# A state-space layer and a feed-forward block on one core: the second half of a matrix is loaded later, and one group of products trades places with another

## The chip, the cores and the metric

The kernel runs on one core of a Trainium2 chip. The metric is the device time of one execution in microseconds (us), the median of several runs. All times along the program are counted from the first instruction of one profiled execution.

## The reference

Sequence length 2048, width 512, 128 states, hidden width 1792, everything in float32. Cut to what matters:

```python
mod = (_silu(c) @ w_mod).reshape(c.shape[0], 6, 1, -1)   # sa, ca, ga, sb, cb, gb
h = _layernorm(x) * (1 + ca) + sa
x = x + ga * _A_ref(h, ...)        # K from A, B, C; y = irfft(rfft(u) * rfft(K)) + u * Dskip
h = _layernorm(x) * (1 + cb) + sb
x = x + gb * _B_ref(h, ...)
...
def _B_ref(x, w1, b1, w2, b2):
    h = x @ w1 + b1
    r = jnp.where(h > 0, h, 0)
    return (r * r) @ w2 + b2
```

So there is first a long convolution along the sequence, by Fourier transforms, and then a feed-forward block with a squared ReLU.

## The kernel before

The kernel has two halves. In the first (to about 283 us) the convolution's filter and the input are brought into the frequency domain and multiplied. In the second, which the change touches, the result is brought back into rows of the sequence and goes through the feed-forward block.

**The inverse.** `inverse(n)` for n of 0 to 7 computes two of the 16 tiles of rows (a tile has 128 rows of 512). TensorE multiplies with matrices in the tile `i2c`: `inverse(n)` reads its blocks 8n to 8n+7, so n of 0 to 3 read the first half of `i2c` (blocks 0 to 31) and n of 4 to 7 the second (32 to 63). The results of `inverse(1)` go to the four PSUM banks `tb` (shown as ps and kg), those of all the others to the four banks `accs` (tg). VectorE adds the input rows (n below 4, line 1106) or VectorE and ScalarE copy the banks (line 1108) into `x2`. `statistics` (lines 1113 to 1118) and `normalised` (ScalarE, line 1124) make the layer norm of a tile, four transposes (line 1129) bring it into banks, and `modulated` (lines 1134 and 1136) scales these into the operands of the feed-forward block.

**The load.** `i2_load(j0, j1, after)` loads blocks j0 to j1 of `i2c` in transfers of eight blocks, 256 KB each. It first lets ScalarE copy one element of `after` into the target (line 991), so that the transfers, which come after this write, cannot begin before `after` is there.

**The first product.** For each pair of 512-row groups (k = 0 and k = 2, with k+1), and for each j of 0 to 6, `first_half` and `second_half` make the products with two column blocks of w1 by seven products in place of eight ("11", "21", "t2", "t3", "t1", "t4", "22"). Each is a call of `three`, six matmuls of float32r parts (lines 1173, 1175 and 1177). `second_half` gets three banks a, c and e; for j of 2 on a is tb[0], c is tb[2], e is tb[3]:

```python
first_half(k, j, tb[0], tb[1], cs_[0])
second_half(k, j, tb[0], tb[2], tb[3], [2 * j - 1, 2 * j])
```

`first_half` writes "11" into tb[0] and copies it to c0 on ScalarE (line 1184). "t2" is then added to what stands in tb[0]. Between the products of t1 and t4 stand two calls of `ffn2`, the products with w2 (lines 1215 to 1217), 12 matmuls each.

**The order.** The order of instructions on each engine is not that of the code. `keep_order` sorts all instructions with a model of their costs and ties them in that order; `hurry(mark, ns)` adds a number of nanoseconds from the table `HURRY` to the urgency of all instructions since `mark`. A changed number, or a changed place in the code, can therefore move other instructions too. TensorE's products that go through `turn` keep the order of the code.

Of the kernel before, what the change touches and what calls it, by code (L numbers as in the profile page):

```python
# [27 lines left out]
def j_of(s, g):  # L28
    return 8 * (s // 2) + 4 * (g // 2) + 2 * (s % 2) + g % 2
# [18 lines left out]
    "GH6H.f..f.fggg.gg.7g.hghhhg"  # L48
).split(".")
HURRY = (  # L50
# [308 lines left out]
def tile_adaln_ssm_ffn(  # L359
# [71 lines left out]
    def in_parts(name, parts):  # L431
        for dst, src in parts:
            whole[nc.sync.dma_start(dst, src).ins.name] = name
# [183 lines left out]
    def hurry(start, ns):  # L617
        urgent.update((i.name, ns) for i in list(nc.cur_bb.bb.instructions)[start:])
# [370 lines left out]
    def i2_load(j0, j1, after):  # L989

        nc.scalar.copy(i2c[:, j0, 0, 0:1], after)
        in_parts(f"inverse {j0}", [(i2c[:, j : j + 8], i2v[:, j : j + 8]) for j in range(j0, j1, 8)])
# [91 lines left out]
    x2 = zj[0].rearrange("p c (s q) d -> p s q c d", q=4)  # L1084
# [3 lines left out]
    def turn(pe):  # L1088
        in_turn.update(x.ins.name for x in pe)

    def inverse(n):
        banks = [t[:, 0:256].rearrange("p (i c d) -> p i c d", i=2, c=NC) for t in (tb if n == 1 else accs)]
        for i in range(2):
            for r in range(2):
                for q in range(4):
                    qs = slice(32 * q, 32 * q + 32)
                    for g in range(4):
                        j = j_of(2 * n + i, g)
                        m = nc.tensor.matmul(  # L1099
                            banks[q][32 * g : 32 * g + 32, i], i2c[qs, j, r], zj[r][qs, :, j],  # L1100
                            start=(r == 0), stop=(r == 1))
                        whole[m.ins.name] = f"inverse {n} {i}"
        for q in range(4):
            y = x2[:, 2 * n : 2 * n + 2, q]
            if n < 4:
                nc.vector.tensor_add(y, cd4[n // 2][:, 2 * (n % 2) : 2 * (n % 2) + 2, q], banks[q])
            else:
                (nc.vector.tensor_copy if q % 2 else nc.scalar.copy)(y, banks[q])

    def statistics(s, n=2):  # L1110
        rs = slice(s, s + n)
        for k in range(s, s + n):
            nc.vector.bn_stats(sts[k % 4], x2[:, k])
            nc.vector.bn_aggr(mv[:, k, :], sts[k % 4])
        nc.scalar.activation(rstd2[:, rs], mv[:, rs, 1], AF.Sqrt, bias=epsb)
        nc.vector.reciprocal(rstd2[:, rs], rstd2[:, rs])
        if on_act(s):
            nc.vector.scalar_tensor_tensor(mv[:, rs, 1], mv[:, rs, 0], -1.0, rstd2[:, rs], op0=ALU.mult, op1=ALU.mult)
# [3 lines left out]
    def normalised(s, xn, tps):  # L1122
        if on_act(s):
            nc.scalar.activation(d4(xn), x2[:, s], AF.Identity, scale=rstd2[:, s : s + 1], bias=mv[:, s, 1:2])
        else:
            nc.vector.tensor_scalar(
                d4(xn), x2[:, s], mv[:, s, 0:1], rstd2[:, s : s + 1], op0=ALU.subtract, op1=ALU.mult)
        m = s % 4
        return [nc.tensor.transpose(tp[:, 128 * m : 128 * m + 128], xn[:, 128 * q : 128 * q + 128], ident) for q, tp in tps]

    def modulated(k, q, tp):
        h = h32[k % 2][:, q]
        if q % 2:
            nc.vector.tensor_scalar(h, tp, cbc[:, q : q + 1], sbc[:, q : q + 1], op0=ALU.mult, op1=ALU.add)
        else:
            nc.scalar.activation(h, tp, AF.Identity, bias=sbc[:, q : q + 1], scale=cbc[:, q : q + 1])
        if k % 2 == 0 or q > 1:
            o = ops[("11", "21", "", "22")[k % 2 * 2 + q // 2]]
            split(o[:, 0, q % 2], o[:, 1, q % 2], h)
# [19 lines left out]
    def squares(k, t, c, src=None):  # L1159
        nc.scalar.activation(c, c if src is None else src, AF.Relu, bias=b1c[:, t : t + 1])  # L1160
        if k % 2:
            nc.scalar.activation(rst[:, t], c, AF.Square)
        else:
            h, l = r2_slot(k, t)
            nc.scalar.activation(h, c, AF.Square)
            nc.scalar.activation(c, c, AF.Square)
            nc.vector.tensor_sub(l, c, h.bitcast(F32))  # L1167

    def three(ps, dst, wi, op, start, stop, on=False):
        o = ops[op]  # L1170
        pe = []
        for kt in range(2):
            pe.append(nc.tensor.matmul(  # L1173
                ps, dst[:, 0, wi, kt], o[:, 0, kt], start=start and kt == 0, stop=False, skip_group_check=on))
            pe.append(nc.tensor.matmul(ps, dst[:, 1, wi, kt], o[:, 0, kt], start=False, stop=False, skip_group_check=on))  # L1175
        for kt in range(2):
            pe.append(nc.tensor.matmul(  # L1177
                ps, dst[:, 0, wi, kt], o[:, 1, kt], start=False, stop=stop and kt == 1, skip_group_check=on))
        turn(pe)
# [9 lines left out]
    def second_half(k, j, a, c, e, between):  # L1189
        dst = sets[j % 2]  # L1190
        c1, c2, c3 = quarters(more[:, 0:2048])[1:]
        t = 2 * j
        three(a, dst, 4, "t2", False, True, True)
        nc.scalar.copy(c1, a)
        three(c, dst, 5, "t3", True, True)
        nc.vector.tensor_add(c3, c1, c)
        three(e, dst, 3, "t1", True, True)
        nc.vector.tensor_add(c3, c3, e)  # L1198
        squares(k + 1, t + 1, c3)
        for n in between:  # L1200
            ffn2(k, n, accs)
        three(c, dst, 2, "t4", False, True, True)
        nc.vector.tensor_add(c2, c1, c)
        squares(k, t + 1, c2)
        three(e, dst, 6, "22", False, True, True)
        nc.vector.tensor_add(c1, c1, e)
        squares(k + 1, t, c1)
# [11 lines left out]
    def ffn2(k, t, to):  # L1219
        n = uses.index((k, t))  # L1220
        w2_ready(n + 2)
        product2(k, t, n, to)
# [23 lines left out]

    mark = len(nc.cur_bb.bb.instructions)
    inverse(0)
    i2_load(32, 64, x2[:, 0, 0, 0, 0:1])
    inverse(1)  # L1250
    for s in range(4):
        if s % 2 == 0:
# [6 lines left out]
    for n in range(2, 8):  # L1259
        if n == 5:  # L1260
            mark = len(nc.cur_bb.bb.instructions)
            for s in range(4, 8):
                if s % 2 == 0:
                    statistics(s)
                normalised(s, xts[s], list(enumerate(accs)))
            for q in range(4):
                modulated(1, q, accs[q])
            hurry(mark, HURRY[49])
            mark = len(nc.cur_bb.bb.instructions)
        inverse(n)  # L1270
        if n in (3, 7):
            hurry(mark, HURRY[6 if n == 3 else 48])
            mark = len(nc.cur_bb.bb.instructions)
# [4 lines left out]
    for k in (0, 2):  # L1278
# [15 lines left out]
        w1_load(2)  # L1294
        w1_load(3)
        second_half(k, 0, tb[0], tb[1], tb[3], [0, 2])
        for _ in w1_set(2, nc.gpsimd):
            pass
        second_half(k, 1, tb[2], tb[1], tb[3], [1])
        for j in range(2, 7):  # L1300
            if j < 6:
                for _ in w1_set(j + 1):
                    pass
            if j < 5:
                w1_load(j + 2)
            if k == 0 and j in (3, 5):
                ss = range(8, 12) if j == 3 else range(12, 16)
                mark = len(nc.cur_bb.bb.instructions)
                for s in ss:
                    nc.sync.dma_start(xos[s % 4], xt[s])  # L1310
                    nc.vector.tensor_add(x2[:, s], x2[:, s], d4(xos[s % 4]))
                    if s % 2:
                        statistics(s - 1)
                hurry(mark, HURRY[55])
            gate_rows(range(4 * k + 2 * j - 4, 4 * k + min(2 * j - 2, 8)))
            first_half(k, j, tb[0], tb[1], cs_[0])
            second_half(k, j, tb[0], tb[2], tb[3], [2 * j - 1, 2 * j])
# [31 lines left out]
        n = uses.index((k + 1, NF - 2))  # L1349
# [59 lines left out]
```

## Time and profile before

| | us |
|---|---|
| runs: median, lowest, highest | 617.12, 617.1, 618.1 |
| the profiled execution | 617.67 |
| its span, first to last instruction | 615.9 |
| TensorE busy in the span | 562.1 |
| VectorE busy | 494.9 |
| ScalarE busy | 418.6 |
| GpSimd busy | 246.7 |

The profile has one line for each engine: PE is TensorE's matmuls, PEld its weight loads, DVE VectorE, ACT ScalarE, POOL GpSimd, SP SyncE, which issues the transfers. A row of the timeline gives start, duration, engine, line, operation, what it writes and reads, the count, and in brackets the idle time before it and what ended that. "issue" stands where an engine waited for nothing that the profile shows. In a row of windows each engine has its busy time and the count of its instructions, then come TensorE's granted clock (1.00 is full speed), the share of the DMA engines that was busy, and GB/s.

### The profile page before, as it was taken

Reading aid. Unit: us, or ns where it says so; the run is one execution under the profiler, and the core shown is the slowest. Engines: PE = TensorE matmul, PEld = TensorE weight load, DVE = VectorE, ACT = ScalarE, POOL = GpSimd, SP = SyncE. Lnnn points to the kernel's source line nnn. Section 1 sums busy time; section 2 is a strip of 40 time slices with the busy share of each in tenths; the row PEclk is TensorE's granted clock in tenths of the full one; section 3 lists DMA queues with packets and bytes.
Section 4 is the critical chain, followed back from the end, with each engine's and each line's share of the span. In section 5 each row is a group of like instructions: output and inputs, shape, how many; then the busy total and the mean of one; then the engine's idle time right before and its main releaser. Section 6 shows DMA issues by size and latency. Waiting matters only on the chain.

```text
span 615.9 us, 21264 instructions
## 1 busy us (share of the span) xinstructions
PE 562.1 (91%) x9238; PEld 484.3 (79%) x9238; DVE 494.9 (80%) x870; ACT 418.6 (68%) x747; POOL 246.7 (40%) x202
## 2 busy tenths in 40 slices
PE   1347998999999999997799999999999999999996
PEld 1235988899899999996677778888888878888885
DVE  6899978999998999945798998547999976654744
ACT  5688869979967678553576866666766766666540
POOL 5549998999998799280004100000000400000000
PEclk9999999999999999998799999999999999999999
DMA  8916041240404401576008131113521532111431
GB/s 307 403 30 202 9 73 31 44 73 4 71 4 72 71 6 27 125 167 224 3 11 278 40 120 35 34 36 99 192 85 55 167 104 69 35 38 40 144 104 69
DMA packets 33133, 57.02 MB, mean 93 GB/s; under 512 B 5520, under 2 KB 14608, under 8 KB 31888
## 3 DMA queue, kind: packets, MB, share of 16 engines
q1 hardware_dynamic: 32752, 55.53, 31.6%
q8 instruction: 72, 1.18, 0.8%
q14 instruction: 21, 0.17, 0.1%
q10 hardware_dynamic: 288, 0.13, 0.1%
HBM read 43.07 MB, written 4.19 MB: 77 GB/s over the span
## 4 chain that ended last, share of the span: by engine, by line
PE 67%; DVE 14%; ACT 9%; issue 4%; DMA 3%; POOL 2%; SPq 1%; DVEq 0%; ACTq 0%; POOLq 0%
PE ps L749 8%; PE ps L903 8%; PE ps L759 7%; PE kg L884 4%; PE ps L1173 4%; PE ps L1175 4%; PE ps L1177 4%; PE tg L1215 3%; PE tg L1217 3%; PE tg L1216 3%; PE tg L1099 2%; PE ps L1217 2%; PE ps L1216 2%; PE ps L1215 2%; DMA work<-w 2%
## 5 line engine op out<-in xcount | busy, mean ns | idle before, releaser
L1036 POOL TENSOR_TENSOR work<-work 128x256 f32<-128x256 f32 x4 | 3.3, 837 | 196.7 <-DVE t2t L1167 134.3
L1010 DVE TENSOR_TENSOR w2t<-rw,w2t 128x512 fp32r<-128x512 f32 x53 | 37.9, 717 | 38.8 <-ACT w2t L1009 38.5
L759 PE MATMUL ps<-xy,t_sb 128*64 128x64 f32 x2048 | 65.9, 223 | 1.0 <-DVE xy L894 1.0
L759 PEld LDWEIGHTS ps<-xy,t_sb 128*64 128x64 f32 x2048 | 63.4, 138 | 2.4 <-DVE xy L894 1.2
L1009 ACT CAST w2t<-rw 128x512 fp32r<-128x512 f32 x53 | 32.8, 619 | 44.6 <-PE kg L1217 21.7
L903 PE MATMUL ps<-e_sb,xy 128*64 128x128 f32 x1024 | 61.0, 274 | 1.9 <-DVE xy L894 1.2
L903 PEld LDWEIGHTS ps<-e_sb,xy 128*64 128x64 f32 x1024 | 56.3, 139 | 3.1 <-DVE xy L894 1.4
L1160 ACT ACTIVATE more<-more,b1c 128x512 f32<-128x512 f32 x54 | 38.9, 720 | 26.4 <-DVE more L1198 15.9
L1215 PE MATMUL tg<-w2t,t2t 128*128 128x512 f32 x112 | 43.9, 392 | 0.5 <-DVE t2t L1167 0.5
L1216 PE MATMUL tg<-w2t,t2t 128*128 128x512 f32 x112 | 43.6, 389 | 0.0
L1217 PE MATMUL tg<-w2t,t2t 128*128 128x512 f32 x112 | 43.6, 389 | 0.0
L894 DVE TENSOR_TENSOR xy<-ps,xy 128x512 f32<-128x512 f32 x64 | 39.9, 681 | 0.5 <-PE ps L759 0.4
L1009 ACT CAST wset<-work 128x512 fp32r<-128x512 f32 (+2 forms) x36 | 24.6, 690 | 22.1 <-DMA work<-w 13.1
L1173 PE MATMUL ps<-opt,wset 128*128 128x512 f32 x84 | 34.1, 405 | 2.4 <-ACT more L1184 2.4
L840 POOL TENSOR_TENSOR llph<-lo,big 128x1024 int32<-128x1024 int32 x16 | 34.3, 2144 | 3.7 <-ACT tg L852 3.6
L840 POOL TENSOR_TENSOR rtlph<-lo,big 128x1024 int32<-128x1024 int32 x16 | 34.4, 2151 | 3.4 <-ACT tg L852 2.8
L749 PE MATMUL ps<-d_sb,ksb 128*64 128x128 f32 x512 | 33.8, 276 | 2.0 <-ACT tg L850 1.4
L1215 PE MATMUL ps<-w2t,t2t 128*128 128x512 f32 x84 | 33.4, 398 | 0.0
L1217 PE MATMUL ps<-w2t,t2t 128*128 128x512 f32 x84 | 32.8, 391 | 0.0
L1175 PE MATMUL ps<-opt,wset 128*128 128x512 f32 x84 | 32.8, 391 | 0.0
L1216 PE MATMUL ps<-w2t,t2t 128*128 128x512 f32 x84 | 32.7, 390 | 0.0
L749 PE MATMUL ps<-d_sb,big 128*64 128x128 f32 x512 | 32.1, 274 | 0.1
(287 smaller groups left out, 1640.1 us busy)
## 6 DMA issues: line engine op xcount, KB each, us to landing
rw<-w SPq DMA_DIRECT2D x53, 256.0 KB, 2.7
xy<-xy SPq DMA_DIRECT2D x64, 128.0 KB, 4.1
xy<-xt SPq DMA_DIRECT2D x24, 256.0 KB, 5.4
work<-w SPq DMA_DIRECT2D x12, 512.0 KB, 4.3
out_dram<-more SPq DMA_DIRECT2D x14, 256.0 KB, 2.2
xy<-w_mod SPq DMA_DIRECT2D x3, 1024.0 KB, 9.9
xy<-w_mod SPq DMA_DIRECT2D x12, 256.0 KB, 3.5
t_sb<-c_t SPq DMA_DIRECT2D x1, 2048.0 KB, 15.3
```

Source lines behind the costliest of these rows:

```text
L749: nc.tensor.matmul(ps[64 * r : 64 * r + 64, 128 * i : 128 * i + 128], src[:, i], d1_sb[:, r], start=True, stop=True)
L759: nc.tensor.matmul(ps[64 * r : 64 * r + 64, 64 * i : 64 * i + 64].rearrange("p (h q t) -> p q h t", h=2, t=2), t2_sb[:, 8 * g + i, r], src ...
L840: nc.gpsimd.tensor_tensor(ph.rearrange("p d r (a b) -> p (d r) a b", a=4), bc(low_phase[:, us].rearrange("p d r b -> p (d r) b"), 2, 4), b ...
L894: nc.vector.tensor_mul(product_piece(y, g), ps, piece(x, g))
L903: nc.tensor.matmul(ps[64 * m : 64 * m + 64, 128 * i : 128 * i + 128], pairs(y)[:, g, i // 2, 64 * m : 64 * m + 64, i % 2], e1_sb[:, h], st ...
L1009: nc.scalar.copy(hi_, raw_)
L1160: nc.scalar.activation(c, c if src is None else src, AF.Relu, bias=b1c[:, t : t + 1])
L1173: pe.append(nc.tensor.matmul(ps, dst[:, 0, wi, kt], o[:, 0, kt], start=start and kt == 0, stop=False, skip_group_check=on))
L1175: pe.append(nc.tensor.matmul(ps, dst[:, 1, wi, kt], o[:, 0, kt], start=False, stop=False, skip_group_check=on))
L1215: nc.tensor.matmul(to[m], l[:, xs], hi_, start=(t == 0), stop=False),
L1216: nc.tensor.matmul(to[m], h[:, xs], lo_, start=False, stop=False),
L1217: nc.tensor.matmul(to[m], h[:, xs], hi_, start=False, stop=(t == NF - 1))])
```

## The change

Two things are moved, and 13 numbers of the table `HURRY` are others (the line with the first two is shown).

```diff
-    ... -627, 3502, 16409, ...
+    ... -627, -53354, 16464, ...
 ...
         t = 2 * j
+        if j > 1:
+            three(c, dst, 5, "t3", True, True)
         three(a, dst, 4, "t2", False, True, True)
         nc.scalar.copy(c1, a)
-        three(c, dst, 5, "t3", True, True)
+        if j < 2:
+            three(c, dst, 5, "t3", True, True)
         nc.vector.tensor_add(c3, c1, c)
 ...
     inverse(0)
-    i2_load(32, 64, x2[:, 0, 0, 0, 0:1])
     inverse(1)
 ...
         inverse(n)
+        if n == 2:
+            i2_load(32, 64, x2[:, 4, 0, 0, 0:1])
         if n in (3, 7):
```

The second half of `i2c` waits for the first sum of `inverse(2)` instead of that of `inverse(0)`. In `second_half`, for j of 2 to 6, the six matmuls of t3 stand ahead of the six of t2. The first of the numbers shown, `HURRY[5]`, is the urgency of `inverse(0)`, `inverse(1)`, and the norm, transposes and scaling of the first four tiles.

On TensorE, in the steps with j of 2 to 6, the end of product 21 (ps_164, the bank tb[1]) was followed by t2 (opt_5427, into ps_163, the bank tb[0]) and then t3 (opt_5426, into ps_165, the bank tb[2]). Before:

```order
L1177 MATMUL ps_164<-op_4746,wset_4635 128x512 x2
L1173 MATMUL ps_163<-opt_5427,wset_4635 128x512
L1175 MATMUL ps_163<-opt_5427,wset_4635 128x512
L1173 MATMUL ps_163<-opt_5427,wset_4635 128x512
L1175 MATMUL ps_163<-opt_5427,wset_4635 128x512
L1177 MATMUL ps_163<-opt_5427,wset_4635 128x512 x2
L1173 MATMUL ps_165<-opt_5426,wset_4635 128x512
```

Now, at the same place of TensorE's program:

```order
L1177 MATMUL ps_164<-op_4746,wset_4635 128x512 x2
L1173 MATMUL ps_165<-opt_5426,wset_4635 128x512
L1175 MATMUL ps_165<-opt_5426,wset_4635 128x512
L1173 MATMUL ps_165<-opt_5426,wset_4635 128x512
L1175 MATMUL ps_165<-opt_5426,wset_4635 128x512
L1177 MATMUL ps_165<-opt_5426,wset_4635 128x512 x2
L1173 MATMUL ps_163<-opt_5427,wset_4635 128x512
```

The six matmuls of t3 have moved between product 21 and t2; it is the same in all ten such steps.

On ScalarE, from the splits of the first blocks of w2 to the scaling of the first operands (xy_95 holds the tiles of rows 0 to 3, xy_91 those of 4 to 7; L991 is the copy that lets the second half of `i2c` go). Before:

```order
L991 COPY i2c<-big_83 128x1
L1009 CAST w2t<-work 128x512
L1115 ACTIVATE rstd_76<-mv_71,epsb 128x2
L1124 ACTIVATE xy_95<-big_83,mv_71,rstd_76 128x512 x2
L1115 ACTIVATE rstd_76<-mv_71,epsb 128x2
L1124 ACTIVATE xy_95<-big_83,mv_71,rstd_76 128x512 x2
L1115 ACTIVATE rstd_76<-mv_71,epsb 128x2
L1136 ACTIVATE work<-ps_163,sbc,cbc 128x512
L1136 ACTIVATE work<-ps_165,sbc,cbc 128x512
L1124 ACTIVATE xy_91<-big_83,mv_71,rstd_76 128x512 x2
```

Now, from the same place:

```order
L1115 ACTIVATE rstd_76<-mv_71,epsb 128x2
L1124 ACTIVATE xy_95<-big_83,mv_71,rstd_76 128x512 x2
L1115 ACTIVATE rstd_76<-mv_71,epsb 128x2
L991 COPY i2c<-big_83 128x1
L1115 ACTIVATE rstd_76<-mv_71,epsb 128x2
L1124 ACTIVATE xy_95<-big_83,mv_71,rstd_76 128x512
L1124 ACTIVATE xy_91<-big_83,mv_71,rstd_76 128x512 x2
L1124 ACTIVATE xy_95<-big_83,mv_71,rstd_76 128x512
L1136 ACTIVATE work<-ps_163,sbc,cbc 128x512
L1115 ACTIVATE rstd_76<-mv_71,epsb 128x2
L1136 ACTIVATE work<-ps_165,sbc,cbc 128x512
```

The copy for the load stands behind the second square root of the statistics (line 1115), and tiles 4 and 5 are scaled ahead of tile 3. On TensorE the transposes of tile 3 still stand ahead of `inverse(4)`, all but the last of the four, which stands behind it now.

6 rows, old and new, of the table HURRY are left out of this document.

## The prediction

> **What bounds the kernel now.** I read the page first (busy shares and the chain), then the table of waits, then the timeline of TensorE (PE) at the two places that the change touches.
>
> ```profile
> span 615.9 us, 21264 instructions
> PE 562.1 (91%) x9238; PEld 484.3 (79%) x9238; DVE 494.9 (80%) x870; ACT 418.6 (68%) x747; POOL 246.7 (40%) x202
> PE 67%; DVE 14%; ACT 9%; issue 4%; DMA 3%; POOL 2%; SPq 1%; DVEq 0%; ACTq 0%; POOLq 0%
> ```
>
> PE is busy for 91% of the span and carries 67% of the chain, so what counts is where it stands still. The table of waits names two such places in the second half of the program:
>
> ```profile
> PEld ps L1173 <- ACT more L1184: 5.6, 10, 1.5
> PEld tg L1099 <- issue: 5.1, 4, 3.6
> PE tg L1099 <- issue: 3.7, 2, 3.1
> ```
>
> The first row is the wait of the products of t2 for ScalarE's copy of c0 (ten of them, one for each `second_half` with j of 2 to 6). The second and third are the inverse, where PE waits for nothing that the profile shows ("issue").
>
> **Part one, t3 ahead of t2.** `second_half` runs the same 36 matmuls in another order, so no work is added or removed. Products of t2 go into the bank tb[0] that product 11 has just filled, and add to it, so they have to wait for the copy of that bank. Products of t3 go into tb[2], which nobody has touched since the step before. These rows of the timeline show the three long waits, and the first and the last of the seven short ones:
>
> ```profile
> 345.30 0.61 PE L1177 MATMUL ps<-op,wset 128*128 128x512 f32 x2
> 345.89 0.57 ACT L1184 COPY more<-ps 128x512 f32<-128x512 f32 x1
> 346.51 0.50 PE L1173 MATMUL ps<-opt,wset 128*128 128x512 f32 x1 [0.59 <-ACT more L1184]
> ...
> 361.15 0.61 PE L1177 MATMUL ps<-op,wset 128*128 128x512 f32 x2
> 361.93 0.56 ACT L1184 COPY more<-ps 128x512 f32<-128x512 f32 x1
> 362.55 0.50 PE L1173 MATMUL ps<-opt,wset 128*128 128x512 f32 x1 [0.79 <-ACT more L1184]
> ...
> 377.19 0.61 PE L1177 MATMUL ps<-op,wset 128*128 128x512 f32 x2
> 377.80 0.50 PE L1173 MATMUL ps<-opt,wset 128*128 128x512 f32 x1
> ...
> 494.79 0.61 PE L1177 MATMUL ps<-op,wset 128*128 128x512 f32 x2
> 495.82 0.56 ACT L1184 COPY more<-ps 128x512 f32<-128x512 f32 x1
> 496.43 0.50 PE L1173 MATMUL ps<-opt,wset 128*128 128x512 f32 x1 [1.03 <-ACT more L1184]
> ...
> 556.50 0.62 PE L1177 MATMUL ps<-op,wset 128*128 128x512 f32 x2
> 556.95 0.42 PE L1173 MATMUL ps<-opt,wset 128*128 128x512 f32 x1
> ```
>
> The pace of PE without waits, the usual length of a matmul, and how busy the other engines are come from these (the columns of the second and third are PE, PEld, DVE, ACT, POOL, then the clock and the DMA share):
>
> ```profile
> L1173 PE MATMUL ps<-opt,wset x84: 389/389/501, 317.9 to 567.0; 128*128 128x512 f32 x84
> 345.00:420.00 75.00, 73.62 (x322) 59.67 (x321) 55.06 (x103) 51.18 (x86) 0.00 (x0) 1.00 0.20 57
> 497.00:571.00 74.00, 74.00 (x325) 60.47 (x324) 43.14 (x69) 48.64 (x80) 0.00 (x0) 1.00 0.19 57
> ```
>
> One matmul takes 74.00/325 = 0.228 us from start to start. At 345.30 two follow each other, so the next was due at 345.76; it came at 346.51, 0.75 late, and lasted 0.50 instead of 0.39: together 0.87 us lost. In the same way 1.06 is lost at 362.55, 1.30 at 496.43, 0.26 at 377.80 and 0.03 at 556.95. The seven short ones together make 0.87 us. The sum is 0.87 + 1.06 + 1.30 + 0.87 = 4.1 us.
>
> With t3 first, six matmuls (1.37 us) stand between the end of product 21 and t2. t2 would then be due at 347.1, 363.0 and 496.6, while the copies end at 346.46, 362.49 and 496.38: slacks of 0.6, 0.5 and 0.2 us. So all ten waits should go. The copy of c1 comes 1.37 us later after this, and so do the two sums into c3; their bank is written again (t4) only behind two calls of `ffn2`, 24 matmuls or 5.5 us, which is their cover; if it were gone, it would cost those 1.37 us at most per step. Bounds for this part: -4.1 us if all goes, 0 if the wait only moves; I take -4.1, since the slacks are positive in all the long ones.
>
> **Part two, the later load.** Four transfers of 256 KB move from behind the first pair of tiles (`inverse(0)`) to behind the third pair (`inverse(2)`). In the places around them the program waits for its own code:
>
> ```profile
> 287.23 1.75 SPq L433 DMA_DIRECT2D i2c<-c_i  x4
> 288.21 0.41 PE L1099 MATMUL ps<-big,i2c 32*32 32x128 f32 x1 [1.51 <-issue]
> 289.15 1.94 PE L1099 MATMUL tg<-big,i2c 32*32 32x128 f32 x76
> 292.12 1.29 DVE L1113 BATCH_NORM_STATS2 st<-big 128x6 f32<-128x512 f32 x2
> 294.23 1.34 PE L1099 MATMUL tg<-big,i2c 32*32 32x128 f32 x43 [3.14 <-issue]
> 295.10 1.60 DVE L1106 TENSOR_TENSOR big<-xy,tg 128x256 f32<-128x256 f32 x4 [1.48 <-PE tg L1099]
> 297.00 1.52 ACT L1124 ACTIVATE xy<-big,mv,rstd 128x512 f32<-128x512 f32 x2 [3.05 <-DVE mv L1118]
> 297.40 2.29 PE L1099 MATMUL tg<-big,i2c 32*32 32x128 f32 x128
> 300.73 1.28 PE L1099 MATMUL tg<-big,i2c 32*32 32x128 f32 x66
> 302.55 1.04 PE L1099 MATMUL tg<-big,i2c 32*32 32x128 f32 x62 [0.53 <-issue]
> 304.77 3.46 PE L1129 MATMUL tg<-ident,xy 128*128 128x128 f32 x16 [1.18 <-DVE big L1108]
> ...
> DMA to landing us min/median/max: 3.1/3.7/4.3
> ```
>
> ```profile
> q8 instruction: 72, 1.18, 0.8%
> ...
> 288.20:291.10 2.90, 2.87 (x127) 2.24 (x128) 2.56 (x9) 1.56 (x3) 0.00 (x0) 0.50 0.87 265
> 288.40:293.30 4.90, 2.68 (x127) 2.06 (x117) 4.53 (x13) 2.43 (x4) 0.00 (x0) 0.50 0.67 216
> 293.30:294.30 1.00, 0.07 (x11) 0.07 (x16) 0.32 (x3) 0.29 (x1) 0.00 (x0) 0.50 0.00 0
> ```
>
> Queue q8 brings 72 pieces of code of 16 KB for PE's 9238 matmuls and 9238 weight loads, one for 257 instructions. Between the two standstills PE ran 127 matmuls and 128 weight loads: one piece. The transfers kept the DMA engines busy until 293.3, and PE went on 0.93 us after that. I read this as the next piece of code standing behind the 1 MB of matrices. The standstills that have no such transfer ahead of them are 1.51 and 0.53 us; the 3.14 should fall between them, and I take 1.0. PE would go on at 292.1 instead of 294.2.
>
> What is late next? VectorE's sums of `inverse(2)` could start 0.87 us later (as 295.10 behind 294.23), but VectorE has its statistics to do first (292.12 + 1.29 + about 0.3): they start at about 293.6 instead of 295.10. They end at 295.2, and `inverse(3)` can begin at 295.3 instead of 297.40. So far 1.5 to 2 us are won. But the new order on ScalarE puts tiles 4 and 5 ahead of tile 3. Tile 2 is scaled from 297.1 (behind a pair of statistics, 1.29, and the small steps, about 0.6), tiles 4 and 5 next, tile 3 last; at 0.76 us each tile 3 is done at 300.2, where it was done at 298.5 (297.00 + 1.52). Its transposes stand in front of `inverse(4)`, which so starts at 300.6 or 300.7, against 300.73. The four transfers now start behind the first sum of `inverse(2)`, at about 294.2, and the first lands 3.1 to 4.3 us later, at 298.5 at most: 2 us before `inverse(4)` reads it. On SP's queue nothing but the load of b2 stands behind them, and that waits for the end of `inverse(7)` in any case. So the gain of 1.5 is nearly all given back; of the rest the standstill of 0.53 may go. Bounds: -1.6 (the whole shift at 295.10 is kept) to +2.6 (first rival); I take -0.3, the end of my walk along the rows.
>
> Other tables move a few steps on ACT and DVE: a weight split or a store ahead of a copy or a gate. Each is 0.4 to 0.7 us on an engine that is not the one waited for, except near 494, where the slack of 0.2 us counts: at most 0.5 us there. I cost it at nothing.
>
> **Sum.** -4.1 - 0.3 = -4.4 us. The profiled execution took 617.67 us (span 615.9 and 1.8 around it), 0.55 above the median of the runs, 617.12. From the profiled one the sum gives 613.3, from the median 612.7; I give the latter. About 0.2% (1.2 us) is what a measurement of this kernel can tell from no change.
>
> **Rivals.**
>
> *The code loses the race again.* In my walk the next piece of code is asked for soon after 292.1 and the transfers are issued at 294.2; they end 6.1 us after their issue (287.23 to 293.30), at 300.3. If that piece falls behind them, `inverse(3)` stops at about 296.6 and goes on at 301.3; it ends near 302.2 instead of 299.6, +2.6: 617.12 - 4.1 + 2.6 = 615.6. For it: that is what the rows above show for the present place. Against it: 2 us between the asking and the issue.
>
> *The standstill stays.* If the matrices were not what delayed the code, PE would go on at 294.2 as now, and only the new order on ScalarE would be left: tile 3 is done about 1.4 us later than now by the same walk, 617.12 - 4.1 + 1.4 = 614.4. For it: PE stands still for 1.51 us at 288.21 also. Against it: the 0.93 us between the end of the transfers and the restart. [...]
>
> *The wait moves on.* ScalarE's copy is late at 346 and 496 because VectorE's sums before it are late; a PE that runs ahead may find VectorE late elsewhere. The three long waits (3.2 us) would come back as others, and the seven short ones and 0.3 would remain: 616.0, no change that can be told. For it: DVE has 14% of the chain. Against it: in 345 to 420 DVE is busy for 55.06 of 75 us and can catch up.
>
> *Slower: the clock stays down.*
>
> ```profile
> 304.70:308.00 3.30, 3.23 (x17) 3.11 (x17) 2.55 (x6) 2.78 (x5) 0.00 (x0) 0.59 0.00 0
> ```
>
> PE's granted clock is 0.50 from 288 to 294 and 0.59 from 304.7 to 308. If the new order feeds it in smaller portions and the half clock lasts into the products behind 308, each microsecond of full-rate work costs one more; it ends slower than now once 5.6 us of such work run so (4.4 + 1.2), and with 8 us of it the time is 620.7. Against it: the products follow each other without a gap from there on. [...]
>
> **How the numbers follow.** Forecast 612.7: 0.53, with a range of its own of 611.4 (the whole -1.6 of part two) to 613.6 (0.9 us of part one left over). The standstill stays 614.4: 0.09. The race 615.6: 0.16, of which 0.03 end within 0.2%. The wait moves on 616.0: 0.15. The clock 620.7: 0.07. Faster is 0.53 + 0.09 + 0.13 = 0.75, the same 0.18, slower 0.07. The range from 610.8 to 616.4 leaves out the clock and the outer edges of the others.
>
> **What would show it.** Right: no wait of L1173 for L1184 in the table; the ten t2 products start 1.37 us behind t3 without a gap; PE's standstill in `inverse(2)` is about 1 us; the 16 transposes start at 304.5 to 304.8. Wrong: a new "issue" standstill of 3 us or more in `inverse(3)`, a wait of PE for VectorE in the ten steps, or transposes before 303.5 or after 306.

## The result, and the profile after

In runs that took turns on one chip, the changed kernel takes 615.14 us (median of 20 runs) and the kernel before 618.13 (20 runs). The ratio is 0.9948, with a 95% interval of 0.9933 to 0.9962: 3.2 us less (2.3 to 4.1). On the base of the prediction, 617.12, that is 613.9, where 612.7 was forecast with a range of 610.8 to 616.4. A second group of runs gave 613.77 against 616.07, 0.9958 (0.9936 to 0.9980).

The page of the changed kernel, the lines that answer to those of before:

```profile
span 613.1 us, 21255 instructions
PE 561.7 (92%) x9238; PEld 485.5 (79%) x9238; DVE 495.6 (81%) x870; ACT 419.8 (68%) x747; POOL 246.1 (40%) x202
PE 72%; DVE 12%; ACT 5%; DMA 4%; issue 2%; POOL 2%; SPq 1%; DVEq 0%; ACTq 0%; POOLq 0%
```

PE's share of the chain went from 67% to 72%, and ScalarE's from 9% to 5%. The table of waits (total us, times, longest):

```profile
PE tg L1099 <- issue: 1.9, 1, 1.9
...
PEld ps L1173 <- ACT more L1184: 1.5, 2, 1.1
...
PE ps L1129 <- ACT xy L1124: 1.0, 1, 1.0
```

Of the ten waits of L1173 for the copy L1184 (5.6 us) two are left (1.5), and the issue standstill in front of tg is 1.9 in place of 3.7. The last row is new: transposes that wait for ScalarE's scaling of tile 3. The timeline of the changed kernel at the steps with t3 ahead of t2 (t3 begins 0.45 us behind the rows of L1177; the rows at 376.99 and 494.37 are its own first matmuls):

```profile
345.62 0.61 PE L1177 MATMUL ps<-op,wset 128*128 128x512 f32 x2
...
346.22 0.57 ACT L1184 COPY more<-ps 128x512 f32<-128x512 f32 x1
...
347.43 0.39 PE L1173 MATMUL ps<-opt,wset 128*128 128x512 f32 x1
...
359.20 0.62 ACT L1009 CAST w2t<-rw 128x512 fp32r<-128x512 f32 x1 [0.95 <-DMA rw<-w]
...
360.58 0.61 PE L1177 MATMUL ps<-op,wset 128*128 128x512 f32 x2
...
362.60 0.56 ACT L1184 COPY more<-ps 128x512 f32<-128x512 f32 x1
...
363.22 0.50 PE L1173 MATMUL ps<-opt,wset 128*128 128x512 f32 x1 [0.67 <-ACT more L1184]
...
376.99 0.39 PE L1173 MATMUL ps<-opt,wset 128*128 128x512 f32 x1
...
378.49 0.50 PE L1173 MATMUL ps<-opt,wset 128*128 128x512 f32 x1
...
494.37 0.39 PE L1173 MATMUL ps<-opt,wset 128*128 128x512 f32 x1
...
494.84 0.57 ACT L1184 COPY more<-ps 128x512 f32<-128x512 f32 x1
...
495.73 0.39 PE L1173 MATMUL ps<-opt,wset 128*128 128x512 f32 x1
```

Behind 345.62 and from 494.37 on the six matmuls of t3 cover the copy, and t2 begins 1.36 us behind t3 without a gap. Behind 360.58 they don't: t2 was due at 362.39 and came at 363.22. The row at 359.20 tells why the copy is late: ScalarE's queue stands behind a cast of w2, and this behind a transfer. The next step (378.49 in place of 378.36) is the other one left.

The timeline at the inverse, from PE's first return after a standstill:

```profile
288.43 0.29 PE L1099 MATMUL ps<-big,i2c 32*32 32x128 f32 x1 [1.41 <-issue]
...
289.04 1.34 PE L1099 MATMUL tg<-big,i2c 32*32 32x128 f32 x80
...
292.29 1.34 PE L1099 MATMUL tg<-big,i2c 32*32 32x128 f32 x43 [1.91 <-issue]
...
294.13 1.38 DVE L1106 TENSOR_TENSOR big<-xy,tg 128x256 f32<-128x256 f32 x4
...
294.77 1.75 SPq L433 DMA_DIRECT2D i2c<-c_i  x4
...
295.46 2.82 PE L1099 MATMUL tg<-big,i2c 32*32 32x128 f32 x128
...
297.33 2.94 ACT L1124 ACTIVATE xy<-big,mv,rstd 128x512 f32<-128x512 f32 x4
...
300.32 0.90 PE L1129 MATMUL ps<-ident,xy 128*128 128x128 f32 x3 [1.00 <-ACT xy L1124]
...
301.16 2.82 PE L1099 MATMUL tg<-big,i2c 32*32 32x128 f32 x128
...
305.69 3.37 PE L1129 MATMUL tg<-ident,xy 128*128 128x128 f32 x16 [1.31 <-DVE big L1108]
```

PE goes on at 292.29 in place of 294.23, and `inverse(3)` begins at 295.46 in place of 297.40: 1.9 us won. But ScalarE scales four tiles in a row and tile 3 last, so PE waits at 300.32, and `inverse(4)` begins at 301.16, where it was 300.73. The 16 transposes begin at 305.69, where it was 304.77.

To see where the time of a whole execution goes, I cut each profile in three: up to the first row of `inverse(0)`; from there to the issue of the load of b2, which waits for the end of `inverse(7)`; and from there to the end. The rows of the load, before and in the changed kernel, are

```profile
321.70 0.33 SPq L1287 DMA_DIRECT2D more<-b  x1
```

```profile
322.49 0.33 SPq L1291 DMA_DIRECT2D more<-b  x1
```

and the three pieces are 283.93, 38.56 and 290.6 us, against 283.61, 38.09 and 294.2 before. The middle piece holds part two of the prediction, the last one part one. So of the 2.8 us between the two profiles -3.6 come from behind `inverse(7)`, +0.5 from the inverse and +0.3 from ahead of it, where nothing was changed. The experiments are told in these pieces, since the times of the runs scatter more than the effects (611.84 to 619.27 for the changed kernel).

| kernel | `inverse(0)` to b2's load | from there to the end | runs: us, ratio to before (95%) |
|---|---|---|---|
| before | 38.09 | 294.2 | 1 |
| the change | 38.56 | 290.6 | 615.14, 0.9948 (0.9933 to 0.9962) |
| the change again | 37.42 | 290.8 | 613.77, 0.9958 (0.9936 to 0.9980) |
| t3 alone | 37.23 | 290.4 | 614.48, 0.9968 (0.9952 to 0.9983) |
| load and table alone | 37.86 | 293.8 | 617.56, 1.0009 (0.9991 to 1.0027) |
| the change, tile 3 first | 36.42 | 290.6 | 612.73, 0.9932 (0.9914 to 0.9951) |
| the change, t1 ahead too | 38.65 | 290.1 | 612.92, 0.9938 (0.9916 to 0.9960) |
| both of these | 36.69 | 289.7 | 611.87, 0.9933 (0.9913 to 0.9952) |
| before, small transfers | 36.09 | 294.4 | 615.72, 0.9989 (0.9968 to 1.0009) |
| t3 alone, small transfers | 36.35 | 290.8 | 613.01, 0.9938 (0.9920 to 0.9956) |
| the change, load behind `inverse(1)` | 49.31 | 289.8 | 623.57, one run |
| the change, load in its old place | 47.51 | 289.0 | 621.18, one run |

The third column falls into two groups: 293.8 to 294.4 wherever t2 stands first, 289.0 to 290.8 wherever t3 does. The second column does not go with that. It scatters by itself, too: with t3 alone nothing is changed in the middle piece, and it is 37.23 in that profile against 38.09.

### The profile page after: what moved, and what is told of

It reads as the page before. It is cut to its first block, busy times and chain, and to the rows that moved or that the text cites. A ratio compares the mean times of both kernels' runs of the same rounds, so it can differ in the third digit from the quotient of the medians.

```text
span 613.1 us, 21255 instructions
## 1 busy us (share of the span) xinstructions
PE 561.7 (92%) x9238; PEld 485.5 (79%) x9238; DVE 495.6 (81%) x870; ACT 419.8 (68%) x747; POOL 246.1 (40%) x202
## 4 chain that ended last, share of the span: by engine, by line
PE 72%; DVE 12%; ACT 5%; DMA 4%; issue 2%; POOL 2%; SPq 1%; DVEq 0%; ACTq 0%; POOLq 0%
PE ps L749 9%; PE ps L759 8%; PE ps L903 7%; PE kg L884 5%; PE ps L1173 4%; PE ps L1175 4%; PE ps L1177 4%; PE tg L1218 4%; PE tg L1219 3%; PE tg L1220 3%; PE ps L1220 3%; PE ps L1219 3%; PE ps L1218 3%; PE kg L1175 2%; PE kg L1173 2%
## 5 line engine op out<-in xcount | busy, mean ns | idle before, releaser
L1010 DVE TENSOR_TENSOR w2t<-rw,w2t 128x512 fp32r<-128x512 f32 x53 | 39.4, 745 | 34.2 <-ACT w2t L1009 34.0
L1173 PE MATMUL ps<-opt,wset 128*128 128x512 f32 x84 | 33.1, 395 | 0.7 <-ACT more L1184 0.7
L1167 DVE TENSOR_TENSOR t2t<-more,t2t 128x512 fp32r<-128x512 f32 x26 | 18.0, 693 | 17.4 <-ACT more L1166 17.2
```

The source lines that it names most:

```text
L1010: eng.tensor_sub(lo_, raw_, hi_.bitcast(F32))
L1173: pe.append(nc.tensor.matmul(ps, dst[:, 0, wi, kt], o[:, 0, kt], start=start and kt == 0, stop=False, skip_group_check=on))
```

## The experiments

The kernels ran in three groups, each beside the kernel before: t3 alone, load and table alone, tile 3 first, and t1 ahead too (before: 617.00 us); both repairs, the change again, and the two other places of the load (616.07); the small transfers (617.11).

### The two parts apart

t3 ahead of t2 alone, with the load and the table of before:

```diff
+        if j > 1:
+            three(c, dst, 5, "t3", True, True)
         three(a, dst, 4, "t2", False, True, True)
         nc.scalar.copy(c1, a)
-        three(c, dst, 5, "t3", True, True)
+        if j < 2:
+            three(c, dst, 5, "t3", True, True)
```

> The kernel before with t3 ahead of t2 alone; the load and the table are the old ones. Theory one (the products bring all of it): 3.0 to 3.6 us below the kernel before, the same time as the whole change; the rows of TensorE show no wait for the copy of c0 except at the second of the ten steps. Rival (the load brings a part): 1.5 to 2.5 us below the kernel before, and above the whole change by 1 us or more. In both, the standstill of about 3 us in inverse(2) is there.

The load and the table alone, with t2 first as before:

```diff
-    ... -627, 3502, 16409, ...
+    ... -627, -53354, 16464, ...
 ...
-    i2_load(32, 64, x2[:, 0, 0, 0, 0:1])
 ...
+        if n == 2:
+            i2_load(32, 64, x2[:, 4, 0, 0, 0:1])
```

> The changed kernel with t2 ahead of t3 again: only the later load and the new table are left. Theory one: within 0.6 us of the kernel before, and the ten waits for the copy of c0 are back at 4 us in all; TensorE goes on in inverse(2) at about 292 instead of 294, but its 16 transposes of tiles 4 to 7 start no earlier than 304.5. Rival: 1 to 2 us below the kernel before.

t3 alone: 614.48 us, 2.0 us below before (1.1 to 3.0). The load and the table alone: 617.56, +0.6 (-0.6 to +1.7), no change that can be told. By its time t3 alone is what the rival had expected (1.5 to 2.5 us), though not by 1 us or more above the whole change: 0.6 to 1.2 by the two ratios. By the pieces it is theory one: the last piece is 290.4 us, as short as in the changed kernel. The waits of the second kernel show that the copy is again in the way:

```profile
PEld ps L1173 <- ACT more L1184: 5.3, 10, 1.2
...
PE ps L1173 <- ACT more L1184: 2.1, 3, 0.8
```

PE's return in `inverse(2)` shows the other side; first t3 alone, then the load and the table alone:

```profile
292.88 1.35 PE L1099 MATMUL tg<-big,i2c 32*32 32x128 f32 x43 [3.28 <-issue]
```

```profile
294.10 1.35 PE L1099 MATMUL tg<-big,i2c 32*32 32x128 f32 x43 [1.22 <-issue]
...
298.39 2.93 ACT L1124 ACTIVATE xy<-big,mv,rstd 128x512 f32<-128x512 f32 x4
...
301.85 1.91 PE L1099 MATMUL tg<-big,i2c 32*32 32x128 f32 x128
```

With the load where it was, the long standstill stays (3.28); with the load moved it is 1.22. PE goes on at 294.10 there and not near 292 as expected, since it came to this piece late, at 290.01; and `inverse(4)` begins no earlier than before, at 301.85. So the gain in the profiles is that of t3; the later load shortens the standstill and gains nothing by it. The runs alone, with their intervals, would leave up to about 1 us open between t3 alone and the whole change.

### Tile 3 ahead of tiles 4 and 5

```diff
-    ... -627, -53354, 16464, ...
+    ... -627, 3502, 16464, ...
```

> The changed kernel with the first changed number of the table at its old value: ScalarE scales tiles 2 and 3 ahead of tiles 4 and 5 again, the load stays late. If the order on ScalarE gives back what the earlier restart won: inverse(4) starts 1 to 1.5 us earlier than in the changed kernel (near 299.7), and the time is 0.5 to 1.3 us below it. Rival (the half clock gives it back): inverse(4) starts earlier but its matmuls and the 16 transposes behind it take as long as in the changed kernel, tiles 6 and 7 come later, and the time is the same within 0.5 us.

612.73 us; by the ratios to before, 0.9932 against 0.9948 and 0.9958, 1.0 to 1.6 us below the changed kernel, inside the intervals. Its timeline:

```profile
295.71 1.52 ACT L1124 ACTIVATE xy<-big,mv,rstd 128x512 f32<-128x512 f32 x2 [1.07 <-DVE mv L1118]
...
299.71 1.28 PE L1099 MATMUL tg<-big,i2c 32*32 32x128 f32 x66
...
301.53 1.04 PE L1099 MATMUL tg<-big,i2c 32*32 32x128 f32 x62 [0.54 <-issue]
```

Two tiles are scaled in one go from 295.71, tile 3 among them, no transposes wait, and `inverse(4)` begins 15.56 us behind `inverse(0)`, where it is 17.23 and 17.08 in the two profiles of the changed kernel and 17.12 in the one before. The middle piece is 36.42 in place of 38.56 and 37.42. So this is where the 1.9 us of the later load went, up to `inverse(4)`: into one number of the table, which puts tiles 4 and 5 first. The same number has moved more: the six matmuls of the first product now stand ahead of the 16 transposes, which begin 21.35 us behind `inverse(0)`, no earlier than the 21.16 of the kernel before. What the middle piece gains behind `inverse(4)` is therefore not due to ScalarE's order alone.

### t1 ahead of t2 as well

```diff
         if j > 1:
             three(c, dst, 5, "t3", True, True)
+            three(e, dst, 3, "t1", True, True)
         three(a, dst, 4, "t2", False, True, True)
 ...
-        three(e, dst, 3, "t1", True, True)
+        if j < 2:
+            three(e, dst, 3, "t1", True, True)
```

> The changed kernel with t1 too ahead of t2, so that 12 matmuls (2.7 us) instead of six stand between product 21 and t2. If the wait that is left at the second step (0.9 us) comes from ScalarE being late by less than 1.4 us there, it goes, and the time is 0.7 to 1.1 us below the changed kernel. Rival (VectorE and ScalarE bound these steps): the wait comes back at another product or at the sums with w2, and the time is the same within 0.5 us.

No wait of L1173 for L1184 is left, and the last piece is 290.1, 0.5 less than in the changed kernel. What was left in the second step was thus ScalarE late by less than six more matmuls. The runs give 612.92, by the ratios 0.6 to 1.2 us below the changed kernel, which is inside the intervals. What is late next on PE is VectorE's operand:

```profile
337.97 0.50 PE L1220 MATMUL tg<-w2t,t2t 128*128 128x512 f32 x1 [0.65 <-DVE t2t L1167]
```

### Both repairs, and the change once more

> The products of t1 also ahead of t2, and tile 3 scaled ahead of tiles 4 and 5: both repairs in one kernel. If the two are independent, it keeps the gain of the later load (about 2 us, all of it ahead of 310 us) and has no wait of L1173 for L1184 (about 0.9 us more): 612.0 us, 0.9 us below the kernel with the repair of tile 3 alone, and 2 to 3 us below the changed kernel. Rival: the saved time meets VectorE's t2 operand (the wait of PE for t2t was 0.41 to 0.65 us in the first steps), and then it is no faster than 612.7 us.

> The changed kernel once more, to be compared with the others of this group on the same chip. Expected 615 us, 0.3 to 0.7% below the kernel before, with one wait of t2 for the copy (L1173 <- L1184) of 0.5 to 0.8 us in the second step of the second half.

Both repairs give 611.87 us, and the changed kernel on the same chip 613.77 (615 was expected): 1.9 us less, the lowest median of all, with runs between 611.26 and 612.94. The changed kernel waits at t2 of the second step again, 0.6 us. Against tile 3 first alone nothing is shown: that ratio was 0.9932, this one is 0.9933. The kernel with both is clearly below the kernel before; against the changed kernel the intervals (0.9913 to 0.9952, and 0.9936 to 0.9980) still overlap. The last piece is 289.7. The middle one is 36.69, no better than with tile 3 first alone, and the timeline has the reason:

```profile
297.92 1.28 PE L1099 MATMUL tg<-big,i2c 32*32 32x128 f32 x66
...
301.01 1.04 PE L1099 MATMUL tg<-big,i2c 32*32 32x128 f32 x62 [1.80 <-issue]
```

`inverse(4)` came early enough to meet a standstill of its own in the middle. The transfers ran from 294.8 to 298.7 there, and the piece of code came in the quarter from 298.75. It is the race of the first rival, at another place.

### Where the code comes

The trace counts the pieces of code (queue q8) in any window, so each piece of PE's code can be found to 0.25 us. In the kernel before, the windows of half a microsecond at the end of the transfers, and the count of q8 between 291.75 and 292.00, are

```profile
291.50:292.00 0.50, 0.00 (x0) 0.00 (x0) 0.50 (x2) 0.47 (x1) 0.00 (x0) 0.50 0.79 275
292.00:292.50 0.50, 0.00 (x0) 0.00 (x0) 0.47 (x2) 0.00 (x0) 0.00 (x0) 0.50 0.02 8
```

```profile
q8 instruction: 1, 0.02, 24.9%
```

The transfers ended at 292.0, not at 293.3 as I had it, and the piece came as they ended. To see whether it waited for them, the kernel before was run with an eighth of the bytes and every instruction in its place; it leaves out seven of eight blocks and uses the eighth in their place, so its values are others. The same was done with t3 ahead:

```diff
-        in_parts(..., [(i2c[:, j : j + 8], i2v[:, j : j + 8]) for j in ...])
+        in_parts(..., [(i2c[:, j : j + w], i2v[:, j : j + w]) for w in [8 if j0 < 32 else 1] for j in ...])
 ...
-    ... i2c[qs, j, r], ...
+    ... i2c[qs, j if j < 32 else j - j % 8, r], ...
```

> The kernel before, with the same instructions in the same order on every engine, but each of the four transfers of the second half brings one block in place of eight, 32 KB in place of 256 KB; inverse(4) to inverse(7) then use one block eight times, so the computed values are others. Theory (the code for PE comes only behind the data that is queued): the piece of code that came 3.5 us after PE's restart in inverse(1) now comes 1.3 to 1.5 us after it, the standstill in inverse(2) falls from 3.14 to 1.2 to 1.9 us, and, with tile 3 scaled ahead of tiles 4 and 5 as before, inverse(4) starts about 15.6 us after inverse(0) in place of 17.12; the time falls by 1 to 2 us, to about 615.5. Rival (the queues take turns, and the standstill has another cause): the piece comes at 3.5 us and the standstill stays at 3 us; no change of the time.

> The same small transfers with t3 ahead of t2 for j of 2 to 6 and all else as before; the computed values are others here too. If the two parts are independent: the gain of t3 first (2.0 us by the runs, 3.4 to 3.8 by the stage behind inverse(7) in the profiles) and that of the small transfers (1 to 2 us) add to 612 us, which bounds from below what any place of the load can give with this order. Rival: nothing over t3 alone, 614.5 us.

Before with small transfers, PE's returns in `inverse(1)` and `inverse(2)`, and `inverse(4)`:

```profile
287.78 0.29 PE L1099 MATMUL ps<-big,i2c 32*32 32x128 f32 x1 [1.41 <-issue]
...
291.92 1.34 PE L1099 MATMUL tg<-big,i2c 32*32 32x128 f32 x43 [1.61 <-issue]
...
299.30 1.90 PE L1099 MATMUL tg<-big,i2c 32*32 32x128 f32 x128
```

The standstill is 1.61 in place of 3.14, and `inverse(4)` begins 16.02 us behind `inverse(0)` in place of 17.12. The piece at this place in all twelve profiles, those with the megabyte ahead of it first:

| kernel | PE goes on | next piece comes (quarter from) | PE goes on with it | between |
|---|---|---|---|---|
| before, transfers behind `inverse(0)` | 288.21 | 291.75 | 294.23 | 6.02 |
| t3 alone, the same place | 287.64 | 290.50 | 292.88 | 5.24 |
| the change, load in its old place | 287.56 | 290.25 | 292.60 | 5.04 |
| before, small transfers | 287.78 | 289.25 | 291.92 | 4.14 |
| t3 alone, small transfers | 287.64 | 289.50 | 292.05 | 4.41 |
| the change | 288.43 | 289.75 | 292.29 | 3.86 |
| both repairs | 287.79 | 289.25 | 291.66 | 3.87 |
| the change again | 287.64 | 289.75 | 292.28 | 4.64 |
| load and table alone | 290.01 | 291.50 | 294.10 | 4.09 |
| the change, tile 3 first | 288.54 | 290.00 | 292.67 | 4.13 |
| the change, t1 ahead too | 287.92 | 289.25 | 291.79 | 3.87 |
| the change, load behind `inverse(1)` | 286.89 | 288.75 | 291.03 | 4.14 |

With little or nothing ahead of it a piece comes 1.3 to 2.4 us after PE has gone on, with the megabyte 2.7 to 3.8. PE uses it 2.0 to 2.7 us after it has come in all twelve. So the large transfers held the piece up here, and there is a floor that the prediction did not have: in the nine profiles without the megabyte ahead 3.9 to 4.6 us pass from one return of PE to the next, where the inverse's small matmuls used the piece up in 1.95 us in the change (288.43 to 290.38, granted clock 1.00) and in 2.88 before (288.21 to 291.09, clock 0.50). It is not always the whole megabyte that a piece waits for: with t3 alone it came at 290.50, and the bulk of the transfers ended near 292.0. PE had gone on 0.35 us after the first of the four was issued there (287.29), with the load in its old place under the new table 0.32 us (287.24), in the kernel before 0.98 us (287.23), and the four take 1.75 us to issue. I read this as a piece that waits for the transfers issued before it is asked for; no run tested that by itself, and a piece that only shares the DMA engines with the transfers is not ruled out. In the runs the small transfers gain 0.7 us (-0.6 to +2.0) alone and, beside t3, 613.01 against 614.48 for t3 alone, on other chips: within what the runs can tell. In the middle piece they gain 2.0 and 0.9 us.

### The load behind the second pair of rows

```diff
     inverse(1)
+    i2_load(32, 64, x2[:, 2, 0, 0, 0:1])
 ...
-        if n == 2:
-            i2_load(32, 64, x2[:, 4, 0, 0, 0:1])
```

> The second half of the inverse's matrices behind the second pair of rows instead of the third; all else as in the changed kernel. Theory (PE's code waits for all data that is already queued): the four transfers now start near 291.5 to 292.5 us and end near 298.6, the piece of code that inverse(3) needs is asked for meanwhile, so PE stands still with issue for 2 to 3 us near 296.7 and goes on near 299.5. Rival (the queues take turns): no issue standstill above 0.6 us in inverse(3), and the first product starts within 0.5 us of where the changed kernel starts it, counted from the start of inverse(0).

```profile
289.45 1.75 SPq L433 DMA_DIRECT2D i2c<-c_i  x4
```

```profile
291.03 1.35 PE L1099 MATMUL tg<-big,i2c 32*32 32x128 f32 x43 [2.18 <-issue]
...
296.42 1.42 PE L1099 MATMUL tg<-big,i2c 32*32 32x128 f32 x52 [0.21 <-issue]
...
317.74 1.73 PE L1099 MATMUL tg<-big,i2c 32*32 32x128 f32 x64 [5.55 <-DVE big L1108]
```

By the number expected, the rival has it: 0.21 us, not 2 to 3. But the transfers began 1 to 2 us earlier than I had assumed. They ran from 290.4 to 294.0, and the next piece behind PE's return at 291.03 came in the quarter from 293.75, at their end, 2.7 to 3.0 us later; PE stood still for it only from 296.2 on. The place of the load decides whether such a wait is seen. The time, 623.57 us, tells nothing of this: with the load here the planner put 64 more matmuls of the inverse ahead of product 21 of the first step, and PE waited 5.55 us for copies at 317.74.

### The load in its old place under the new table

```diff
     inverse(0)
+    i2_load(32, 64, x2[:, 0, 0, 0, 0:1])
     inverse(1)
 ...
-        if n == 2:
-            i2_load(32, 64, x2[:, 4, 0, 0, 0:1])
```

> The load back behind the first pair of rows, but with the changed table and t3 ahead of t2. Theory (the later load wins about 2 us in inverse(2), the table's order of ScalarE gives them back): PE stands still for 3 us or more in inverse(2), and tile 3 is scaled last, so the 16 transposes start 22.5 us or later after the start of inverse(0) (21.76 in the changed kernel). Rival (the table costs nothing): the transposes start by 21.0 us, as with t3 alone (20.62).

```profile
292.60 1.35 PE L1099 MATMUL tg<-big,i2c 32*32 32x128 f32 x43 [2.32 <-issue]
...
296.89 2.93 ACT L1124 ACTIVATE xy<-big,mv,rstd 128x512 f32<-128x512 f32 x4
...
301.53 0.55 PE L1129 MATMUL ps<-ident,xy 128*128 128x128 f32 x3
...
317.03 1.72 PE L1099 MATMUL tg<-big,i2c 32*32 32x128 f32 x64 [5.56 <-DVE big L1108]
```

A miss: 621.18 us, a standstill of 2.32, and transposes from 20.4 us behind `inverse(0)` on, as the rival had it. ScalarE scales four tiles in a row, tile 3 behind tiles 4 and 5 as in the changed kernel, but with the load here PE's transposes of tile 3 (301.53) stand behind `inverse(4)`, which began at 299.50 and so did not wait for them. Later 5.56 us are lost by the same order as above. The run leaves open what the table costs by itself; it shows that with another place of the load the same table gives another order on PE.

## Why the prediction was right, point by point

**t3 ahead of t2, -4.1: the mechanism right, the size 0.3 to 0.7 too large.** Eight of ten waits went, and t2 follows t3 after 1.36 or 1.37 us, as forecast. Lost are 0.83 + 0.11 = 0.94 us at 363.22 and 0.13 + 0.11 = 0.24 at 378.49, so 2.9 of the 4.1 came. The last piece fell by 3.4 to 3.8 in the three profiles with t3 alone or the change; I did not find all of the rest; 0.35 of it is the first product with w2, which stood 0.62 us behind VectorE's t2t at 337.46 in the profile before and came 0.27 late, at 337.78, in this one. The step that failed is "all ten waits should go". It took the end of the copy in the second step as 362.49, from the profile before. The copy ended at 363.16, since ScalarE waits there for a transfer of w2 (359.20, 0.95), which was issued at 355.91, as VectorE's row of L1010 that read its buffer had ended at 355.83. The slack of 0.5 against a row that stands behind a DMA was none here. The t1 experiment bears that out.

**The later load, -0.3: each step of the walk right, up to the clock.** PE went on at 292.29 (forecast 292.1), `inverse(3)` began at 295.46 (295.3), VectorE's sums stood at 294.13 (293.6), and tile 3 was done at 300.27 (300.2). That ScalarE's new order gives back what the load wins was the main claim here, and the kernel with tile 3 first shows it at the start of `inverse(4)`: 15.56 us behind `inverse(0)` in place of 17.23 and 17.08. The standstill was 1.91, not 1.0, since PE did the piece before it in 1.34 instead of 1.94 us and then waited for the same moment. The wrong step was the transposes: 305.69, not 304.5 to 304.8. It is the clock, as these windows show, of the kernel before, of the change, and of the change in its second profile:

```profile
298.00:305.00 7.00, 5.27 (x250) 3.94 (x233) 5.88 (x20) 5.28 (x12) 0.00 (x0) 0.97 0.02 5
```

```profile
298.00:305.00 7.00, 5.38 (x154) 3.52 (x136) 4.45 (x12) 5.73 (x11) 0.00 (x0) 0.50 0.17 63
```

```profile
298.00:305.00 7.00, 4.68 (x163) 3.57 (x147) 5.71 (x15) 6.12 (x12) 0.00 (x0) 0.98 0.07 27
```

The granted clock was 0.97 before, 0.50 in this execution of the change and 0.98 in the other one. At half clock `inverse(4)` takes 2.82 us, at full clock 1.90. In the second profile the transposes begin 20.76 us behind `inverse(0)`, which is 304.4 on the prediction's scale. So part two is +0.5 in the one and -0.7 in the other, and nothing that the runs can tell; that the forecast's -0.3 lies between them is luck, since the clock moves this piece by more than that (`inverse(4)` alone by 0.92).

**The reason given for the standstill was right, its reading wrong.** "The transfers kept the DMA engines busy until 293.3" came from one window of 4.9 us; they ended at 292.0. That the piece stood behind them held all the same: with an eighth of the bytes it came 2.1 us sooner behind PE's return. The price of the race was counted with the same 293.3, so its 300.3 was too late. How much of the transfers a piece waits for the rows do not settle: two pieces came as the transfers ended (in the quarters from 291.75, before, and from 293.75, with the load behind `inverse(1)`), and one, with t3 alone, about 1.3 us ahead of their end (in the quarter from 290.50, with the bulk of them ended near 292.0).

**The rivals.** The race was not lost in `inverse(3)`, which shows no issue standstill in the changed kernel; in the kernel with both repairs it was lost in `inverse(4)` (1.80). The standstill did not stay, though 1.91 us of the 3.14 did. The third rival had the waits come back elsewhere on PE: what is left, 1.2 us, is at t2 itself. The clock did stay down in one profile, at 0.50 for 17.1 us (291.5 to 308.6), on a stretch ahead of the one that I had priced, though PE was busy for 14.0 us of it; the two profiles of the change are 1.1 us apart in the middle piece.

## To carry to other kernels

A wait on a bank that was just copied can go when work on another bank stands between, as eight of ten did here; count the cover against the latest end of the copy, behind its own transfers, not against its end in one profile. A gain at one standstill counts at the next meeting point: here 1.9 us of PE's time ended in a queue on ScalarE, and one number of the planner's table decided whether it was kept up to `inverse(4)`. A large transfer issued ahead of an engine's next piece of code is worth a look where a piece is used up in 2 to 3 us, as by PE in the inverse: here it delayed the piece by about 2 and 1 us in the two pairs of kernels with and without the bytes.

## What the runs showed of the hardware

- Around the inverse, half clock (a granted clock of 0.50) came in stretches of 3.4 us or multiples of it: 10.2 and 3.4 us before, 17.1 in the change, 10.2 and 3.4 in its second profile. The first began 7.6 us behind `inverse(0)` in one execution of the change and 4.7 in the other.
- The times of the changed kernel went with the mean granted clock: of its 20 runs the three lowest (611.84 to 612.67 us) have 0.990 to 0.993, the two highest (618.19 and 619.27) 0.970 and 0.969. A change of 1 us is seen sooner in a stage of the profile than in the median.
- PE took 2.0 to 2.7 us from the arrival of a piece of its code to the first matmul behind a standstill, in all twelve profiles, with a megabyte of other transfers under way or without.
